# A spectral filter and a gated MLP in one kernel: the order of the first loads and the place of column 1's transposes

## The chip, the cores and the metric

The kernel runs on one core of a Trainium2 chip. The metric is device time in microseconds (us) of one execution; smaller is better. Each kernel is run several times and the median is given.

## The reference

What has to be computed, cut to its core (x is 2048 x 512 in bf16, w_gate and w_up are 512 x 1792, w_down 1792 x 512, w_r and w_i 2048 x 257):

```python
xn = _layernorm(x, axis=-1)
X = rfft2(xn); X = X * (w_r + 1j * w_i); a = irfft2(X)      # spectral branch
g = xn @ w_gate; u = xn @ w_up; b = (gelu_tanh(g) * u) @ w_down   # gated branch
return x + a + b
```

## The kernel before, in words

The 2048 rows are held as 16 "columns" of 128 rows: column c has the rows 16 p + c, p being the partition (`x_v`). For each column VectorE takes the statistics (`f_stats`, L337, `f_mean`, L340), the reciprocal root comes from ScalarE and VectorE for columns 0 and 1 and from GpSimd for the others, and the normalised xn goes to two places: transposed into `xnT` for the gated branch, and as it is into the spectral branch. Columns 0 to 3 are transposed on TensorE (`f_T`, L349) and copied from PSUM (`f_Tc`, L352); columns 4 to 15 are transposed by DMA (L450).

The gated branch is cut into units (`unit`). A unit has some columns and one to four blocks of 128 features: gate matmuls into `g_ps`, up matmuls into `u_ps`, a gelu on ScalarE (L498), a product on VectorE (L503) that writes `hT`. Each of the matmuls contracts 128 of the 512 inputs; e = 0..3 counts these. Units 0 and 1 are columns 0 and 1 with features 0 to 511, units 2 and 3 are columns 0 and 1 together with features 512 to 1023, then come columns 2 and 3, then all of columns 0 to 3 for the other features (`todo`). Unit 0 has its matmuls in halves over e, so that it can start on half of the weights (`mm_half`, L493); all other units are in `mm` (L485). Down products (`y_ps`, L815) make up the last third of the span. The spectral branch (`forward`, `group`, `inverse`: groups bp, dp, ep, gp, yp) is set between the units.

The order of the work on TensorE, VectorE, ScalarE, GpSimd and most of SyncE comes from a planner (`Plan.order`): each operation has an engine, an estimated length, what it depends on, a key (lower goes first when several could start), and in some cases an earliest time, `t_min`. The tables `LAND`, `WG_LAND` and `WU_LAND` give the planner such earliest times for the loads. Buffers are counted by names ("S", "G", "U" and so on: G and U have two PSUM buffers each, S has four). The planner only sets the order of instructions on each engine; on the chip they wait for each other by semaphores. The first loads and the filler matmuls are written out by hand in `opening`.

In `opening`, SyncE issues columns 0 and 1, four loads of the first up weights (features 0 to 511, one for each e), columns 2-3, the second gate and up weights (features 512 to 1023), columns 4-7, the third weights, columns 8-11, the table RF, columns 12-15, a small index table `idx_t` and constants. ScalarE issues the first gate weights in two halves. A DMA uses one of eight semaphores in turn, so the ninth load in order waits until the first has landed, the tenth until the second has, and so on. Column 0 goes through VectorE and TensorE (two transposes, filler matmuls L322, ScalarE's copies) to unit 0. Column 1 is made ready while unit 0 runs; its four transposes stand behind unit 0's up matmuls on TensorE, one VectorE copy takes all of them to `xnT`, and unit 1 comes next. ScalarE loads the gelu's table after the root of column 1. Of `first_two`, the statements for column 1's transposes:

```python
t = add("PE", 0.23, lambda: f_T(1, 0, NE), [o["xn1"]], key=-1998, lat=0.45, acq=("S",))
v("copyt", lambda: f_Tc(1, 0, NE), 0.5, ["t"])
xT_op[1] = o["copyt"]
return o["copyt"]
```

Of the kernel before, what the change touches and what calls it, by code (L numbers as in the profile page):

```python
# [21 lines left out]
NE = 4  # L22
# [179 lines left out]
def kernel(  # L202
# [50 lines left out]
    def load_x(c0, n, eng=nc.sync):  # L253
        eng.dma_start(out=x_t[:, c0:c0 + n, :], in_=x_v[:, c0:c0 + n, :])

    def load_w(a, b, eng=nc.sync):
        nc.sync.dma_start(out=Wg_sb[:, :, a:b], in_=wg_v[:, :, a:b])
        eng.dma_start(out=Wu_sb[:, :, a:b], in_=wu_v[:, :, a:b])
# [15 lines left out]
    def opening():  # L274
        nc.vector.memset(spin[:], 0.0)
        nc.vector.memset(eps_t[:], EPS)
        nc.vector.memset(minus_half[:], -0.5)
        U = nc.gpsimd
        U.memset(ident_t[:], 1.0)
        U.affine_select(out=ident_t[:], in_=ident_t[:], pattern=[[-1, P]], compare_op=ALU.is_equal, fill=0.0,  # L280
                        base=0, channel_multiplier=1)
        nc.scalar.activation(out=warm[:], in_=eps_t[:], func=AF.Sqrt, bias=eps_t[:], scale=1.0)
        load_x(0, 1)
        load_x(1, 1)
        load_w(Wg_sb, 0, 512, nc.scalar, e=slice(0, 2))
        load_w(Wg_sb, 0, 512, nc.scalar, e=slice(2, 4))
        for e in range(NE):
            load_w(Wu_sb, 0, 512, e=e)
        load_x(2, 2)
        load_w(Wg_sb, 512, 1024)  # L290
        load_w(Wu_sb, 512, 1024)
        load_x(4, 4)
        load_w(Wg_sb, 1024, DF)
        load_w(Wu_sb, 1024, DF)
        load_x(8, 4)
        nc.sync.dma_start(out=RF_t[:], in_=rf_d.rearrange("p (c k) -> p c k", c=NC))
        load_x(12, 4)
        nc.sync.dma_start(out=idx_t[:], in_=nc.inline_tensor(idx_np, name="spec_rows").ap())
        load_consts("F0", "L0")
        load_consts("I0", "M0")  # L300
        for T, w_in in ((TR, A_w_r), (TI, A_w_i)):
            rows = w_in.rearrange("(kb a h g) k -> h kb a (g k)", kb=NC, h=2, a=8)
            Tf = T.rearrange("p j k -> p (j k)")
            for h in range(2):
                nc.sync.dma_start(out=Tf[64 * h:64 * h + 64, W:8 * W], in_=rows[h, :, 0:4, W:8 * W])
        for k in range(37):
            nc.tensor.matmul(sp_ps[:, :P], lhsT=spin[:], rhs=spin[:], start=True, stop=True)  # L307

    LAND = {0: 2.9, 1: 4.5, 2: 7.2, 3: 7.2}
    LAND.update({c: 11.5 if c < 8 else 17.5 if c < 12 else 20.5 for c in range(4, NC)})  # L310
    WG_LAND = [5.0] * 4 + [8.6] * 4 + [13.2] * 6
    WU_LAND = [6.7] * 4 + [10.0] * 4 + [15.2] * 6
    RF_LAND = 19.0

    ident = ident_t[:]
# [35 lines left out]
    def f_Tc(c, e0, n, copy=V.tensor_copy):  # L351
        copy(out=xnT[0][:, e0:e0 + n, c, :], in_=tiles["T", c, e0][:])  # L352
# [14 lines left out]
        U.tensor_tensor(out=b, in0=mv[:, c0:c0 + n, 0], in1=rstd[:, c0:c0 + n], op=ALU.mult)  # L367
        U.tensor_scalar(out=b, in0=b, scalar1=-1.0, scalar2=None, op0=ALU.mult)  # L368

    xn_op, xT_op = {}, {}  # L370

    def first_two():
        o = {}

        def v(k, fn, occ, deps=(), lat=None, t_min=0.0):
            o[k] = add("DVE", occ, fn, [o[d] for d in deps], key=-2000 + len(o), lat=lat, t_min=t_min,
                       after=o.get("last"))
            o["last"] = o[k]

        def T(c, h):  # L380
            o["T", c, h] = add("PE", 0.12, lambda: f_T(c, 2 * h, 2), [o["xn", c, h]], key=-2000 + 2 * c + h,
                               lat=0.36, acq=("S",))

        def xn_(c, h):
            v(("xn", c, h), lambda: f_norm_v(c, 256 * h, 256), 0.27, [("recip", c)], lat=0.4)

        def stats(c):
            v(("stats", c), lambda: f_stats(c), 0.6, t_min=LAND[c], lat=0.7)

        def mean(c):  # L390
            v(("mean", c), lambda: f_mean(c), 0.17, [("stats", c)])
            o["root", c] = add("ACT", 0.31, lambda: A.activation(
                out=rstd[:, c:c + 1], in_=mv[:, c, 1:2], func=AF.Sqrt, bias=eps_t[:], scale=1.0),
                [o["mean", c]], key=-2000 + c)

        def recip(c):
            v(("recip", c), lambda: V.reciprocal(out=rstd[:, c:c + 1], in_=rstd[:, c:c + 1]), 0.15, [("root", c)])

        stats(0)
        mean(0)  # L400
        recip(0)
        xn_(0, 0)
        xn_(0, 1)
        stats(1)
        mean(1)
        T(0, 0)
        T(0, 1)
        add("PE", 0.33, spin_on, [o["T", 0, 1]], key=-1500, lat=0.33, after=o["T", 0, 1])
        table = add("ACT", 1.3, lambda: None, [o["root", 1]], key=-1500, lat=1.3)
        xT_op[0, 0], xT_op[0] = (  # L410
            add("ACT", 0.36, lambda h=h: f_Tc(0, 2 * h, 2, A.copy), [o["T", 0, h]], key=-1990 + h, lat=0.48,
                rel=("S",)) for h in range(2))
        recip(1)
        xn_op[0] = o["xn", 0, 1]
        v("xn1", lambda: f_norm_v(1, 0, D), 0.33, [("recip", 1)], lat=0.45)
        t = add("PE", 0.23, lambda: f_T(1, 0, NE), [o["xn1"]], key=-1998, lat=0.45, acq=("S",))
        o["t"] = t
        v("copyt", lambda: f_Tc(1, 0, NE), 0.5, ["t"])
        o["copyt"].rel = ("S",)
        xT_op[1] = o["copyt"]  # L420
        xn_op[1] = o["xn1"]
        return o["copyt"]

    ROOT = 1.1
    chain_end = first_two()
# [39 lines left out]
    def unit(k, c0, n, f0, m=1):  # L465
# [19 lines left out]
                    T_.matmul(b[name][:, f], lhsT=W_[:, e, (f0 + f) * P:(f0 + f + 1) * P], rhs=rhs[:, e, :],  # L485
                              start=(e == 0), stop=(e == NE - 1))

        def mm_half(s, name="g_ps", tag="G", W_=Wg_sb):
            if s == 0:
                b[name] = ps.tile([P, m, w], F32, name=name, tag=tag, bufs=2)  # L490
            for e in (2 * s, 2 * s + 1):
                for f in range(m):
                    T_.matmul(b[name][:, f], lhsT=W_[:, e, (f0 + f) * P:(f0 + f + 1) * P], rhs=rhs[:, e, :],  # L493
                              start=(e + f == 0), stop=(e == NE - 1), skip_group_check=True)
# [12 lines left out]
        def split(name, tag, W_, key, t, h):  # L507
# [3 lines left out]
                        lat=occ * h / m + 0.3, acq=() if f else (tag,), t_min=t[f0 + f + h - 1])  # L511
            return o

        if k == 0:
            g = add("PE", occ / 2, lambda: mm_half(0), [xT_op[0, 0]], key=1000, acq=("G",), t_min=WG_LAND[0])
            g = add("PE", occ / 2, lambda: mm_half(1), [xT_op[0], g], key=1000.1, lat=occ / 2 + 0.3)
            u = add("PE", occ / 2, lambda: mm_half(0, "u_ps", "U", Wu_sb), [g], key=1000.5, acq=("U",), t_min=6.2)
            u = add("PE", occ / 2, lambda: mm_half(1, "u_ps", "U", Wu_sb), [u], key=1000.6, lat=occ / 2 + 0.3,
                    t_min=WU_LAND[0])
        else:  # L520
            g = split("g_ps", "G", Wg_sb, 1000 + k, WG_LAND, m)
            u = split("u_ps", "U", Wu_sb, 1000.5 + k, WU_LAND, (2, m, 1)[k] if k < 3 else m)
        ge = add("ACT", {1: 0.28, 2: 0.36, 4: 0.5}[n * m], f_ge, [g], key=-1000 + k,
                 lat={1: 0.38, 2: 0.48, 4: 0.7}[n * m], acq=("ge",), rel=("G",))
        h = add("DVE", {1: 0.21, 2: 0.34, 4: 0.61}[n * m], f_h, [ge, u], key=-1000 + k, rel=("U", "ge"))
# [354 lines left out]
```

## Time and profile before

| What | us |
|---|---|
| Median of 6 runs | 178.9 (178.81 to 179.15) |
| The profiled execution, its own time | 178.81 |
| Its span in the profile | 177.1 |
| TensorE busy | 171.9 (97%) |
| VectorE busy | 115.6 (65%) |
| ScalarE busy | 96.4 (54%) |
| GpSimd busy | 17.1 (10%) |
| TensorE share of the chain that ended last | 95% |

The span goes from the first to the last instruction in the profile; the 1.7 us between it and the execution's time lie around it. The "chain" is the run of work that ended last, followed back from the last instruction to what released each step. A line of the chain has a start and a length in us, the engine, the tile written, the line of the kernel and how many instructions were merged. A line of the timeline has the same with shapes added, and in brackets how long the engine was idle before, and what ended the wait. SPq and ACTq are DMA issues on SyncE's and ScalarE's queues; "us to landing" of a DMA counts from the start of its issue to the moment at which a waiting engine can go on. TensorE ran at its full granted clock in the whole span by the page (clock tenths 9 throughout).

### The profile page before, as it was taken

What the parts mean: (1) busy time and instruction counts of PE and PEld (TensorE: products, weight loads), DVE (VectorE), ACT (ScalarE), POOL (GpSimd) and SP (SyncE); (2) the same over time, 40 slices, a digit from 0 to 9 for tenths busy, and PEclk for the clock granted to TensorE, in tenths of its full rate; (3) what the DMA queues carried; (4) which work ended last, traced back from release to release, by engine and by line L of the source; (5) the groups of instructions that cost most, each with busy time, mean ns of one, the idle gap of its engine ahead of it and who ended that gap; (6) DMA issues with size and microseconds to landing.
All of it is one profiled execution on the core that took longest, in us unless ns stands there. A gap on an engine that the chain in (4) does not pass through costs nothing.

```text
span 177.1 us, 3114 instructions
## 1 busy us (share of the span) xinstructions
PE 171.9 (97%) x1128; PEld 97.4 (55%) x1145; DVE 115.6 (65%) x253; ACT 96.4 (54%) x172; POOL 17.1 (10%) x38
## 2 busy tenths in 40 slices
PE   7999999999999999999999999999999999999993
PEld 7898845464545554555555444454445445444463
DVE  2588799988334599998799999543516325345333
ACT  4633389798745999799999955452112111211200
POOL 1020260406760000000000000000000000000000
PEclk9999999999999999999999999999999999999999
DMA  5999975543717802111201520200132221221212
GB/s 151 324 365 401 349 165 97 112 92 51 246 33 236 297 4 59 43 46 35 59 14 47 146 68 0 59 0 4 57 91 89 75 76 61 89 87 61 79 43 59
DMA packets 21359, 19.35 MB, mean 109 GB/s; under 512 B 8480, under 2 KB 20000, under 8 KB 21344
## 3 DMA queue, kind: packets, MB, share of 16 engines
q1 hardware_dynamic: 20384, 17.31, 33.3%
q0 software_dynamic: 416, 1.32, 2.6%
q10 hardware_dynamic: 544, 0.52, 1.1%
q8 instruction: 9, 0.15, 0.3%
q14 instruction: 6, 0.05, 0.1%
HBM read 13.38 MB, written 2.10 MB: 87 GB/s over the span
## 4 chain that ended last, share of the span: by engine, by line
PE 95%; DMA 1%; issue 1%; DVE 1%; SPq 0%
PE y_ps L815 27%; PE u_ps L485 27%; PE g_ps L485 25%; PE sp_ps L307 2%; PE yp L766 2%; PE bp L575 2%; PE dp L633 2%; PE y_ps L819 2%; PE gp L736 2%; PE ep L642 2%; DMA F<-F 1%; PE tp L349 1%; PE g_ps L493 1%; PE u_ps L493 1%; PE sp_ps L322 0%
## 5 line engine op out<-in xcount | busy, mean ns | idle before, releaser
L485 PE MATMUL u_ps<-xnT,Wu_sb 128*128 128x512 bf16 (+2 forms) x254 | 56.5, 349 | 0.3
L485 PE MATMUL g_ps<-xnT,Wg_sb 128*128 128x512 bf16 (+2 forms) x246 | 55.2, 348 | 0.8 <-DVE xnT L352 0.5
L815 PE MATMUL y_ps<-Wd_sb,hT 128*128 128x512 bf16 (+2 forms) x247 | 50.5, 355 | 0.2
L503 DVE TENSOR_TENSOR hT<-u_ps,ge 128x512 bf16<-128x512 f32 x56 | 38.5, 688 | 18.4 <-PE u_ps L485 14.1
L498 ACT ACTIVATE ge<-g_ps 128x512 bf16<-128x512 f32 x56 | 33.8, 604 | 22.0 <-PE g_ps L485 18.1
L815 PEld LDWEIGHTS <-hT 128*128 128x128 bf16 x252 | 23.2, 98 | 22.5
L485 PEld LDWEIGHTS <-Wu_sb 128*128 128x128 bf16 x256 | 24.0, 98 | 20.9
L485 PEld LDWEIGHTS <-Wg_sb 128*128 128x128 bf16 x256 | 23.8, 98 | 20.5 <-issue 0.6
L772 ACT CAST yf<-yp 128x512 bf16<-128x512 f32 x16 | 9.3, 586 | 40.5 <-PE yp L766 40.5
L822 DVE TENSOR_TENSOR y_sb<-y_ps,y_sb 128x512 bf16<-128x512 f32 (+2 forms) x18 | 11.1, 631 | 30.0 <-PE y_ps L819 30.0
L647 ACT CAST E<-ep 64x512 bf16<-64x512 f32 x32 | 18.5, 579 | 1.3 <-PE ep L642 0.8
L337 DVE BATCH_NORM_STATS2 stats<-x_t 128x6 f32<-128x512 bf16 x16 | 10.5, 678 | 3.0 <-DMA x_t<-in_A_x_dram 3.0
L447 ACT ACTIVATE xn<-x_t,nb,rstd 128x512 bf16<-128x512 bf16 x12 | 9.5, 814 | 2.1 <-POOL nb L368 2.1
L545 ACT CAST Gs<-gp 128x512 bf16<-128x512 f32 x16 | 9.0, 593 | 1.0 <-PE gp L736 0.9
L545 ACT CAST ds<-dp 128x512 bf16<-128x512 f32 x16 | 9.0, 598 | 0.6 <-PE dp L633 0.5
L545 ACT CAST Bs<-bp 128x512 bf16<-128x512 f32 x16 | 8.6, 608 | 0.5 <-PE bp L575 0.5
L778 DVE TENSOR_TENSOR lv<-yf 128x512 bf16<-128x512 bf16 x16 | 6.1, 421 | 1.5 <-ACT yf L772 0.6
L766 PEld LDWEIGHTS <-Gs 128*128 128x128 bf16 x64 | 4.8, 98 | 3.5
L785 DVE TENSOR_TENSOR yt<-lv 128x512 bf16<-128x512 bf16 x16 | 6.1, 422 | 0.3
L766 PE MATMUL yp<-CT,Gs 128*128 128x128 bf16 x64 | 6.0, 219 | 0.1
L819 PE MATMUL y_ps<-yt,RI_t 128*128 128x512 bf16 (+2 forms) x18 | 6.1, 355 | 0.0
L736 PEld LDWEIGHTS <-F 128*128 128x128 bf16 x64 | 4.5, 98 | 2.6
(67 smaller groups left out, 124.2 us busy)
## 6 DMA issues: line engine op xcount, KB each, us to landing
F<-F SPq DMA_DIRECT2D x32, 64.0 KB, 2.0
y_sb<-in_A_x_dram SPq DMA_DIRECT2D x16, 128.0 KB, 2.1
out_dram<-y_sb SPq DMA_DIRECT2D x15, 128.0 KB, 1.7
Wd_sb<-in_B_w_down_dram SPq DMA_DIRECT2D x1, 1792.0 KB, 7.9
x_t<-in_A_x_dram SPq DMA_DIRECT2D x3, 512.0 KB, 11.7
Wg_sb<-in_B_w_gate_dram SPq DMA_DIRECT2D x1, 768.0 KB, 9.0
Wu_sb<-in_B_w_up_dram SPq DMA_DIRECT2D x1, 768.0 KB, 10.5
Wg_sb<-in_B_w_gate_dram ACTq DMA_DIRECT2D x2, 256.0 KB, 3.8
```

The lines of the kernel that those rows point to most:

```text
L337: V.bn_stats(out=st[:], in_=x_t[:, c, :])
L447: xn_op[c] = add("ACT", 0.72, lambda c=c: A.activation(out=xn[:, c, :], in_=x_t[:, c, :], func=AF.Identity, bias=nb[:, c:c + 1], scale=rst ...
L485: T_.matmul(b[name][:, f], lhsT=W_[:, e, (f0 + f) * P:(f0 + f + 1) * P], rhs=rhs[:, e, :], start=(e == 0), stop=(e == NE - 1))
L498: A.activation(out=b["ge"][:], in_=b["g_ps"][:], func=AF.Gelu_apprx_tanh)
L503: V.tensor_tensor(out=hT_of(sb, f0, m, o, w), in0=b["u_ps"][:], in1=b["ge"][:], op=ALU.mult)
L545: A.copy(out=o, in_=i)
L647: A.copy(out=b["E"][64 * h:64 * h + 64, r], in_=b["ep", h][64 * r:64 * r + 64])
L766: T_.matmul(t[:, q], lhsT=late["G"][:, q, c0 + j], rhs=IQ[q], start=(q == 0), stop=(q == 3), skip_group_check=True)
L772: A.copy(out=b["yf"][:, j], in_=b[j][:])
L815: T_.matmul(b[o][:], lhsT=hT_of(sb, f, 1, cl * P, P)[:, 0], rhs=Wd_sb[:, f, o:o + w], start=(f == 0), stop=False)
L819: T_.matmul(b[o][:], lhsT=late["RI"][:, c, :], rhs=late["yt"][:, c, o:o + w], start=False, stop=True)
L822: V.tensor_tensor(out=b["y"][:, o:o + w], in0=b[o][:], in1=b["y"][:, o:o + w], op=ALU.add)
```

## The change

First, in `opening`: the first up weights go to ScalarE's queue, in two halves as the gate weights, and columns 2-3 behind them on that queue. SyncE issues columns 0 and 1, then `idx_t`, then the second gate weights. Ahead of that load GpSimd copies one element of column 0 to the first place that the load will write, so that the load waits for the copy, and the copy for column 0. Columns 8 to 15 come in four loads of two instead of two of four.

Second, in `first_two` and `unit`: column 1's transposes are in two pairs, and stand between the first and the second quarter of unit 0's up matmuls. VectorE copies the first pair, ScalarE the second pair, ahead of its table load. Unit 1's gate has halves over e too, so that its first half needs VectorE's copy only.

Third, the planner's landing estimates for columns 0 and 1 and for the up weights are other numbers.

```diff
--- before.py
+++ after.py
@@ -282,20 +282,22 @@
         nc.scalar.activation(out=warm[:], in_=eps_t[:], func=AF.Sqrt, bias=eps_t[:], scale=1.0)
         load_x(0, 1)
         load_x(1, 1)
-        load_w(Wg_sb, 0, 512, nc.scalar, e=slice(0, 2))
-        load_w(Wg_sb, 0, 512, nc.scalar, e=slice(2, 4))
-        for e in range(NE):
-            load_w(Wu_sb, 0, 512, e=e)
-        load_x(2, 2)
+        for T in (Wg_sb, Wu_sb):
+            for e in (0, 2):
+                load_w(T, 0, 512, nc.scalar, e=slice(e, e + 2))
+        load_x(2, 2, nc.scalar)
+        nc.sync.dma_start(out=idx_t[:], in_=nc.inline_tensor(idx_np, name="spec_rows").ap())
+        U.tensor_copy(out=Wg_sb[0:1, 0, 512:513], in_=x_t[0:1, 0, D - 1:D])
         load_w(Wg_sb, 512, 1024)
         load_w(Wu_sb, 512, 1024)
         load_x(4, 4)
         load_w(Wg_sb, 1024, DF)
         load_w(Wu_sb, 1024, DF)
-        load_x(8, 4)
+        load_x(8, 2)
+        load_x(10, 2)
         nc.sync.dma_start(out=RF_t[:], in_=rf_d.rearrange("p (c k) -> p c k", c=NC))
-        load_x(12, 4)
-        nc.sync.dma_start(out=idx_t[:], in_=nc.inline_tensor(idx_np, name="spec_rows").ap())
+        load_x(12, 2)
+        load_x(14, 2)
         load_consts("F0", "L0")
         load_consts("I0", "M0")
         for T, w_in in ((TR, A_w_r), (TI, A_w_i)):
@@ -306,10 +308,10 @@
         for k in range(37):
             nc.tensor.matmul(sp_ps[:, :P], lhsT=spin[:], rhs=spin[:], start=True, stop=True)
 
-    LAND = {0: 2.9, 1: 4.5, 2: 7.2, 3: 7.2}
+    LAND = {0: 2.65, 1: 4.6, 2: 7.2, 3: 7.2}
     LAND.update({c: 11.5 if c < 8 else 17.5 if c < 12 else 20.5 for c in range(4, NC)})
     WG_LAND = [5.0] * 4 + [8.6] * 4 + [13.2] * 6
-    WU_LAND = [6.7] * 4 + [10.0] * 4 + [15.2] * 6
+    WU_LAND = [6.4] * 4 + [10.2] * 4 + [15.2] * 6
     RF_LAND = 19.0
 
     ident = ident_t[:]
@@ -367,7 +369,7 @@
         U.tensor_tensor(out=b, in0=mv[:, c0:c0 + n, 0], in1=rstd[:, c0:c0 + n], op=ALU.mult)
         U.tensor_scalar(out=b, in0=b, scalar1=-1.0, scalar2=None, op0=ALU.mult)
 
-    xn_op, xT_op = {}, {}
+    xn_op, xT_op, between = {}, {}, {}
 
     def first_two():
         o = {}
@@ -413,13 +415,17 @@
         recip(1)
         xn_op[0] = o["xn", 0, 1]
         v("xn1", lambda: f_norm_v(1, 0, D), 0.33, [("recip", 1)], lat=0.45)
-        t = add("PE", 0.23, lambda: f_T(1, 0, NE), [o["xn1"]], key=-1998, lat=0.45, acq=("S",))
-        o["t"] = t
-        v("copyt", lambda: f_Tc(1, 0, NE), 0.5, ["t"])
-        o["copyt"].rel = ("S",)
-        xT_op[1] = o["copyt"]
+        o["t", 0] = add("PE", 0.12, lambda: f_T(1, 0, 2), [o["xn1"]], key=1000.54, lat=0.3, acq=("S",))
+        o["t", 1] = add("PE", 0.12, lambda: f_T(1, 2, 2), [o["xn1"]], key=1000.55, lat=0.3, acq=("S",),
+                        after=o["t", 0])
+        between.update(o)
+        v("copyt0", lambda: f_Tc(1, 0, 2), 0.25, [("t", 0)], lat=0.4)
+        o["copyt1"] = add("ACT", 0.4, lambda: f_Tc(1, 2, 2, A.copy), [o["t", 1], table], key=-1400)
+        o["copyt0"].rel = o["copyt1"].rel = ("S",)
+        xT_op[1, 0] = o["copyt0"]
+        xT_op[1] = o["copyt1"]
         xn_op[1] = o["xn1"]
-        return o["copyt"]
+        return o["copyt0"]
 
     ROOT = 1.1
     chain_end = first_two()
@@ -485,10 +491,10 @@
                     T_.matmul(b[name][:, f], lhsT=W_[:, e, (f0 + f) * P:(f0 + f + 1) * P], rhs=rhs[:, e, :],
                               start=(e == 0), stop=(e == NE - 1))
 
-        def mm_half(s, name="g_ps", tag="G", W_=Wg_sb):
-            if s == 0:
+        def mm_part(e0, e1, name="g_ps", tag="G", W_=Wg_sb):
+            if e0 == 0:
                 b[name] = ps.tile([P, m, w], F32, name=name, tag=tag, bufs=2)
-            for e in (2 * s, 2 * s + 1):
+            for e in range(e0, e1):
                 for f in range(m):
                     T_.matmul(b[name][:, f], lhsT=W_[:, e, (f0 + f) * P:(f0 + f + 1) * P], rhs=rhs[:, e, :],
                               start=(e + f == 0), stop=(e == NE - 1), skip_group_check=True)
@@ -511,15 +517,21 @@
                         lat=occ * h / m + 0.3, acq=() if f else (tag,), t_min=t[f0 + f + h - 1])
             return o
 
+        up = "u_ps", "U", Wu_sb
         if k == 0:
-            g = add("PE", occ / 2, lambda: mm_half(0), [xT_op[0, 0]], key=1000, acq=("G",), t_min=WG_LAND[0])
-            g = add("PE", occ / 2, lambda: mm_half(1), [xT_op[0], g], key=1000.1, lat=occ / 2 + 0.3)
-            u = add("PE", occ / 2, lambda: mm_half(0, "u_ps", "U", Wu_sb), [g], key=1000.5, acq=("U",), t_min=6.2)
-            u = add("PE", occ / 2, lambda: mm_half(1, "u_ps", "U", Wu_sb), [u], key=1000.6, lat=occ / 2 + 0.3,
-                    t_min=WU_LAND[0])
+            g = add("PE", occ / 2, lambda: mm_part(0, 2), [xT_op[0, 0]], key=1000, acq=("G",), t_min=WG_LAND[0])
+            g = add("PE", occ / 2, lambda: mm_part(2, NE), [xT_op[0], g], key=1000.1, lat=occ / 2 + 0.3)
+            u = add("PE", occ / 4, lambda: mm_part(0, 1, *up), [g], key=1000.5, acq=("U",))
+            between["t", 0].deps.append(u)
+            u = add("PE", occ / 4, lambda: mm_part(1, 2, *up), [u, between["t", 1]], key=1000.6)
+            u = add("PE", occ / 2, lambda: mm_part(2, NE, *up), [u], key=1000.7, lat=occ / 2 + 0.3, t_min=WU_LAND[0])
+        elif k == 1:
+            g = add("PE", occ / 2, lambda: mm_part(0, 2), [xT_op[1, 0]], key=1001, acq=("G",))
+            g = add("PE", occ / 2, lambda: mm_part(2, NE), [*src, g], key=1001.3, lat=occ / 2 + 0.3)
+            u = split(*up, 1001.5, WU_LAND, m)
         else:
             g = split("g_ps", "G", Wg_sb, 1000 + k, WG_LAND, m)
-            u = split("u_ps", "U", Wu_sb, 1000.5 + k, WU_LAND, (2, m, 1)[k] if k < 3 else m)
+            u = split("u_ps", "U", Wu_sb, 1000.5 + k, WU_LAND, 1 if k == 2 else m)
         ge = add("ACT", {1: 0.28, 2: 0.36, 4: 0.5}[n * m], f_ge, [g], key=-1000 + k,
                  lat={1: 0.38, 2: 0.48, 4: 0.7}[n * m], acq=("ge",), rel=("G",))
         h = add("DVE", {1: 0.21, 2: 0.34, 4: 0.61}[n * m], f_h, [ge, u], key=-1000 + k, rel=("U", "ge"))
```

## The prediction, made before the changed kernel ran

> **What bounds the kernel now.** First view: the page's busy shares and its chain. TensorE is busy 97% of the span and holds 95% of the chain that ended last, so time comes off only where TensorE waits. Second view: the chain from 5 us, which shows where that is.
>
> ```profile
> 5.60 0.64 PE sp_ps L322 x6
> 6.24 1.07 PE g_ps L493 x16
> 7.31 0.89 PE u_ps L493 x16
> 8.20 0.24 PE tp L349 x4
> 8.44 0.02 issue
> 8.46 0.44 DVE xnT L352
> 8.90 0.04 issue
> 8.94 1.05 PE g_ps L485 x16
> 10.00 0.89 PE u_ps L485 x16
> 10.89 0.87 PE g_ps L485 x8
> 11.76 0.87 PE u_ps L485 x8
> 12.64 0.45 PE tp L349 x8
> ```
>
> Columns: start, length, what. Between 8.44 and 8.94 TensorE has transposed column 1 and stands still until VectorE has copied it: 0.50 us. From 8.94 it never stops for more than 0.05 us until the tail. Ahead of 6.24 it runs filler matmuls (37, then 6), whose number is fixed, so an earlier column 0 gains nothing.
>
> Third view: SyncE's part of the timeline, with the times from issue to landing of the DMA list. Issue plus landing time gives when each load is usable.
>
> ```profile
> 3.60 0.43 SPq L266 DMA_DIRECT2D x_t<-in_A_x_dram  x1
> 4.74 0.39 SPq L270 DMA_DIRECT2D Wg_sb<-in_B_w_gate_dram  x1
> 5.93 0.38 SPq L270 DMA_DIRECT2D Wu_sb<-in_B_w_up_dram  x1
> ```
>
> ```profile
> Wg_sb<-in_B_w_gate_dram SPq DMA_DIRECT2D x1, 512.0 KB, 5.3
> Wu_sb<-in_B_w_up_dram SPq DMA_DIRECT2D x1, 512.0 KB, 5.6
> x_t<-in_A_x_dram SPq DMA_DIRECT2D x1, 256.0 KB, 4.5
> ```
>
> Columns 2-3 land at 3.60 + 4.5 = 8.1, the second gate weights at 4.74 + 5.3 = 10.04, the second up weights at 5.93 + 5.6 = 11.53. The chain needs the last two at 10.89 and 11.76: spare 0.85 and only 0.23 us. This is the number to keep: the stall hides a DMA that is nearly late too.
>
> Fourth view: VectorE and ScalarE in the same stretch.
>
> ```profile
> 8.81 1.28 DVE L337 BATCH_NORM_STATS2 stats<-x_t 128x6 f32<-128x512 bf16 x2
> 10.00 0.30 DVE L340 BATCH_NORM_AGGREGATE mv<-stats 128x2 f32<-128x6 f32 x2
> 10.22 1.48 DVE L503 TENSOR_TENSOR hT<-u_ps,ge 128x512 bf16<-128x512 f32 x2
> 11.61 0.73 DVE L343 TENSOR_SCALAR xn<-x_t,mv,rstd 128x512 bf16<-128x512 bf16 x2
> ```
>
> ```profile
> 6.28 1.28 ACT L498 ACT_TABLE_LOAD   x1
> 7.58 0.60 ACT L498 ACTIVATE ge<-g_ps 128x512 bf16<-128x512 f32 x1
> ```
>
> VectorE works without a gap from the statistics of columns 2-3 (8.81) to their normalised form (12.34); TensorE transposes them at 12.64 to 13.08, so that chain has about 0.2 us to spare: its last xn is ready 3.53 after the statistics start, then come a hand-over (0.06), four transposes (0.22) and their lag (0.3), so statistics that start at s let the transposes end at s + 4.1 at the earliest.
>
> **What the skill says.** "DMA: Bandwidth & Descriptors", section "Issuing engines are not separate DMA queues": loads issued from several engines run on the same 16 DMA engines; only issue time is saved. The trace agrees: the core's rate from 4 to 7 us is 338 to 384 GB/s, with both queues active at first and SyncE's alone later. Same page, "Queues, rings and completion order": each DMA engine takes the queues in turn, packet by packet. The packet records agree: from 3.5 to 5.0 us the SyncE queue moved 231 KB and the ScalarE queue 283, 45 to 55. So moving a load to the other queue doesn't give it more bandwidth, it decides with whom it shares. No other place of the skill is used.
>
> **The change part by part.**
>
> *Column 1 inside the first up unit.* The same 4 transposes now follow 4 of the 16 up matmuls: 7.31 + 4 x 0.056 = 7.53, so they end at 7.77. xn of column 1 is ready at 6.91, 0.6 before. The copy is in two halves: VectorE's (the 512-wide one took 0.42, a half on ScalarE 0.33; I take 0.3) from 7.79 to 8.1, ScalarE's from 7.8 to 8.13. Meanwhile TensorE has 12 up matmuls left: 7.77 + 0.67 = 8.44. Gate of unit 1 starts there and not at 8.94: **-0.50 us**, hidden by those 0.67 us. If Wu e=2..3 is late the cover stretches with the stall.
>
> *ScalarE's copy ahead of the table load.* The load moves from 6.28 to 8.13-9.41; the first gelu ends at 10.02 and not at 8.18. Behind it wait the second gelu (10.6), the first product on VectorE (10.05, was 10.22, so no later) and the PSUM slot of unit 2's gate, wanted at 10.89 - 0.50 = 10.39: 0.3 spare. Cost 0; if the copy were 0.4 later, it would show on TensorE.
>
> *Two up weights, then columns 2-3 on ScalarE's queue.* Three more issues of about 0.48 after 2.03 end at 3.46; the next ScalarE work is at 3.92. Cost 0. They are issued at 2.0, 2.5, 3.0 instead of 1.71 to 3.60, behind the same bytes. Wu e=2..3 is wanted at 8.0 (landed 6.9 before).
>
> *idx_t first.* SyncE has it as third load: 1.5 KB in 128 rows. Its packets took 9 ns each, so 128/16 x 9 = 0.07 us of each DMA engine at least; at most as long as preparing 128 rows of any load: the first packet of column 1 came 0.92 us after that of the 256-row Wg load issued before it, hence 0.46 for 128 (estimate). All later loads move by 0.07 to 0.46.
>
> *The hold.* The GpSimd copy of one element: the same shape at L597 took 0.70 us. It waits for column 0 (2.97), so SyncE's gate load goes out at about 3.8, instead of 4.74; behind it on SyncE are all later loads, each of them before held by an older load's semaphore anyway. Queued on GpSimd behind it is the root of columns 2-3 (10.39), long after. The earlier issue can close the dip at 7 to 8 us (239 GB/s against about 370): up to 0.33 us earlier for what follows. But it can also share with Wu and columns 2-3: see the second rival.
>
> *x in pairs (8-15), key changes in the planner.* These columns are wanted from 13.7 on by VectorE and at 33 by TensorE: 0. On TensorE the order of some units with bp, dp, ep groups changes further on (the compiled order of both kernels shows it); every group stays between units of 0.87 us, and no stall over 0.05 shows there now: -0.1 to +0.5, taken as 0.
>
> **Sum.** Unit 2's up starts at the later of 11.76 - 0.50 = 11.26 and the landing of the second up weights, 11.53 shifted by -0.26 (dip closed, cheap idx) to +0.46. I take +0.05, as both effects are of like size: 11.58. The stall goes, and 0.32 of it comes back as a wait for Wu. Gain 11.76 - 11.58 = 0.18. The chain of columns 2-3 allows it: landing at 8.1 to 8.5, transposes end at 12.6 at best; TensorE's own end 12.90. TensorE is full after that, so the 0.18 lasts. The profiled execution took 178.81, span 177.1 plus 1.7 outside, unchanged: 178.63. The median of the runs is 178.90, 0.09 above: **178.7** (178.72).
>
> **Rivals.** *Full gain*: the dip closes and idx costs little; Wu lands at 11.27, 0.49 to 0.50 come off: 178.4. For: GpSimd frees SyncE 0.9 us earlier. Against: the DMA engines are already over 90% busy in all but that one microsecond.
>
> *Columns 2-3 come late (slower)*: with the gate load on SyncE's queue from about 3.8 + 1.05 = 4.9 (column 0: issue 0.80, first packet 1.84), ScalarE's queue gets 55% of 366 KB/us = 201. Up to 4.9, 552 of its 1,280 KB are through; the rest needs 3.6 us: 8.5, plus 0.5 to 0.75 from last data to usable: 9.0 to 9.3. Then the transposes end at 9.25 + 4.1 = 13.35 instead of 13.08: +0.27, with Wu e=2..3 about 7.9, just in time: 179.2, up to 179.5. It decides from a landing of 9.0. For: the 45 to 55 sharing. Against: column 1, issued at 1.22, moved nothing until 3.24, while a ScalarE load issued before it did: loads seem to be prepared in order of issue, and then the gate load stays behind columns 2-3.
>
> *The new order further on* exposes a wait at a group (ScalarE is over 95% busy from 80 to 100 us): +0.5, 179.4.
>
> **Numbers.** Forecast 46%, full gain 19%, columns 2-3 late 25%, later order 10%. A measurement tells about 0.2% (0.36 us) from no change: faster is below 178.54, slower above 179.26. Faster: 0.14 x 46 + 0.9 x 19 = 24%. Slower: 0.03 x 46 + 0.6 x 25 + 0.9 x 10 = 25%, and 3 more for the unpriced waits: 28%. Same: 48%. The range takes the full gain less a little (178.35) to the late columns with +0.45 (179.35).
>
> **What would show it.** Right: gate of unit 1 at about 8.44 with no wait for xnT; a gap of 0.2 to 0.4 before unit 2's up, ended by the Wu DMA; statistics of column 2 by 8.5. Wrong: gap before Wu e=2..3 (7.99), statistics waiting for the x DMA past 9.0, or a gate of unit 2 waiting for gelu; gaps on TensorE past 20 us.

## The result and the profile after

| | before | after |
|---|---|---|
| Median, us | 179.12 (178.60 to 180.02, 69 executions) | 179.67 (178.91 to 180.72, 32) |
| Ratio, 95% interval | 1 | 1.003 (1.002 to 1.0039) |
| The profiled execution, us | 178.81 | 179.51 |
| Its span, us | 177.1 | 177.5 |
| Execution less span, mean of all executions, us | 1.70 | 1.95 |

The changed kernel is slower by 0.54 us (0.003 x 179.12), where 0.18 less was forecast. The last row says that 0.25 of it lies outside the span; the other 0.29 is inside. The two profiled executions differ by more, 0.4 in the span: that of the kernel before is a quick one, 0.31 below its median. Inside, the chain of the changed kernel, followed back from 14 us:

```profile
4.86 7.13 DMA Wu_sb<-in_B_w_up_dram
11.99 0.05 issue
12.04 1.05 PE u_ps L491 x8
13.08 0.45 PE tp L351 x8
```

Before, this stretch was TensorE all the way but for the copy of `xnT`. Now one load, the second up weights, fills it from its issue at 4.86 to 11.99. The chain has the up matmuls of unit 2 at 12.04 where they stood at 11.76, and 1.05 long where they were 0.87. That is two ways of counting: behind another group the chain counts a group only from the end of the one ahead, which it overlaps; after a wait it counts all of it. TensorE's timeline, which counts every group from its own start, has the group 1.04 and 1.05 long, from 11.60 before and from 12.04 after:

```profile
11.60 1.04 PE L485 MATMUL u_ps<-xnT,Wu_sb 128*128 128x256 bf16 x8
```

So the group is late by 0.44, and the transposes of columns 2-3 end at 13.53 and not at 13.08. From the start of this group to TensorE's last matmul it is 162.5 us in both kernels, and in all runs below but e7, e10 and e11: what is lost ahead of this start is the loss. The timeline of the changed kernel has the waits in brackets:

```profile
8.07 0.62 PE L499 MATMUL u_ps<-xnT,Wu_sb 128*128 128x128 bf16 x8 [0.33 <-DMA Wu_sb<-in_B_w_up_dram]
8.52 1.06 PE L499 MATMUL g_ps<-xnT,Wg_sb 128*128 128x128 bf16 x16
10.60 1.03 PE L491 MATMUL g_ps<-xnT,Wg_sb 128*128 128x256 bf16 x8
12.04 1.05 PE L491 MATMUL u_ps<-xnT,Wu_sb 128*128 128x256 bf16 x8 [0.40 <-DMA Wu_sb<-in_B_w_up_dram]
```

The wait for `xnT` is gone, as meant. In its place are two waits for DMAs, one for the second half of the first up weights and one for the second up weights. A third gap, 0.13 us ahead of unit 2's gate at 10.60, has no releaser in the profile; the second gate weights land just before it. SyncE's timeline and the list of DMAs (last column: us from issue to landing) give the landings:

```profile
3.43 0.40 SPq L270 DMA_DIRECT2D Wg_sb<-in_B_w_gate_dram  x1
4.86 0.38 SPq L270 DMA_DIRECT2D Wu_sb<-in_B_w_up_dram  x1
```

```profile
Wg_sb<-in_B_w_gate_dram SPq DMA_DIRECT2D x1, 512.0 KB, 7.1
Wu_sb<-in_B_w_up_dram SPq DMA_DIRECT2D x1, 512.0 KB, 7.1
...
x_t<-in_A_x_dram ACTq DMA_DIRECT2D x1, 256.0 KB, 6.1
```

The second weights are issued 1.3 and 1.1 us earlier than before and land 0.5 and 0.4 later: 3.43 + 7.1 = 10.53 and 4.86 + 7.1 = 11.96. (The chain, which is exact, has 11.99 for the last; the list rounds to 0.1.) Columns 2-3 (issued at 3.10) land at 9.20, 1.1 later. The windows of both kernels show it in sums (first columns: window, its length, TensorE busy; last: DMA share, GB/s), first before, then after:

```profile
4.50:6.50 2.00, 2.00 (x22) 2.00 (x20) 1.50 (x6) 1.05 (x4) 0.00 (x0) 1.00 1.10 385
6.20:13.10 6.90, 6.38 (x95) 6.05 (x93) 4.67 (x12) 3.34 (x6) 0.97 (x2) 1.00 1.00 333
13.10:20.00 6.90, 6.90 (x65) 6.19 (x64) 5.27 (x13) 2.77 (x5) 0.00 (x0) 1.00 1.05 398
```

```profile
4.50:6.50 2.00, 2.00 (x28) 1.64 (x26) 1.57 (x6) 0.92 (x3) 0.00 (x0) 1.00 1.08 322
6.20:13.10 6.90, 6.04 (x86) 5.19 (x84) 4.29 (x11) 3.55 (x6) 0.97 (x2) 1.00 1.04 363
13.10:20.00 6.90, 6.90 (x69) 6.22 (x67) 5.64 (x14) 2.70 (x5) 0.00 (x0) 1.00 1.05 384
```

TensorE's idle time between 6.2 and 13.1 us goes from 0.52 to 0.86, which is the three gaps (0.33, 0.13, 0.40). The DMA rate is lower in the first window and higher in the second, and from 13.1 us TensorE is busy throughout in both kernels.

### The profile page after: what moved, and what is told of

The parts are those of the page before. It is cut to its first block, busy times and chain, and to the rows that moved or that the text cites. A ratio compares the mean times of both kernels' runs of the same rounds, so it can differ in the third digit from the quotient of the medians.

```text
span 177.5 us, 3118 instructions
## 1 busy us (share of the span) xinstructions
PE 171.9 (97%) x1127; PEld 96.7 (54%) x1145; DVE 115.7 (65%) x253; ACT 96.9 (55%) x173; POOL 17.4 (10%) x39
## 4 chain that ended last, share of the span: by engine, by line
PE 91%; DMA 6%; issue 1%; SPq 0%; DVE 0%
PE y_ps L827 27%; PE u_ps L491 26%; PE g_ps L491 26%; DMA Wu_sb<-in_B_w_up_dram 4%; PE gp L748 2%; PE yp L778 2%; DMA x_t<-in_A_x_dram 2%; PE bp L587 2%; PE dp L645 2%; PE y_ps L831 2%; PE ep L654 2%; PE tp L351 0%; SPq L266 0%; DVE y_sb L834 0%
## 5 line engine op out<-in xcount | busy, mean ns | idle before, releaser
L491 PE MATMUL u_ps<-xnT,Wu_sb 128*128 128x512 bf16 (+2 forms) x248 | 55.6, 348 | 0.8 <-DMA Wu_sb<-in_B_w_up_dram 0.4
L491 PE MATMUL g_ps<-xnT,Wg_sb 128*128 128x512 bf16 (+1 forms) x236 | 55.0, 357 | 0.3
L491 PEld LDWEIGHTS <-Wg_sb 128*128 128x128 bf16 x240 | 23.0, 98 | 20.8 <-issue 0.3
L569 DVE TENSOR_TENSOR A<-xn 128x1024 bf16<-128x1024 bf16 x8 | 5.2, 676 | 1.0 <-ACT xn L453 1.0
```

## The experiments

Each run changes the kernel before or after in one part. A ratio is to the kernel before, run beside it on the same chip. "Outside" is the execution less its span. "End" is the time from VectorE's last product (`y_sb`) to the last instruction of the profiled execution. "Rest" is the ratio's difference in us less what these two differ from 1.70 and 2.45: an estimate of what happens in the work itself. A ratio is known to 0.2 to 0.5 us either way, so small entries mean little. Issue and landing times are those of one profiled execution each, to 0.05 us, and it can lie far from the median (e10: 182.20 against 180.33; e9: 179.28 against 179.95).

| Kernel | Ratio (95%) | Outside, us | End, us | Rest, us | Second gate, up issued | Columns 2-3 land | Second up lands |
|---|---|---|---|---|---|---|---|
| before | 1 | 1.70 | 2.45 | 0 | 4.74, 5.93 | 8.10 | 11.53 |
| after | 1.003 (1.002 to 1.0039) | 1.95 | 2.45 | +0.29 | 3.43, 4.86 | 9.20 | 11.96 |
| e1 | 0.9985 (0.9975 to 0.9996) | 1.70 | 2.45 | -0.27 | 5.03, 6.18 | 7.90 | 11.78 |
| e2 | 1.0023 (1.0011 to 1.0035) | 1.96 | 2.45 | +0.15 | 3.87, 4.66 | 8.41 | 11.66 |
| e4 | 1.0023 (1.0003 to 1.0043) | 1.96 | 2.45 | +0.15 | 3.26, 3.69 | 10.31 | 12.69 |
| e6 | 1.0032 (1.0019 to 1.0045) | 1.71 | 2.57 | +0.44 | 3.20, 3.70 | 8.99 | 12.00 |
| e9 | 1.0045 (1.0034 to 1.0056) | 1.72 | 2.57 | +0.67 | 3.20, 3.68 | 8.79 | 11.88 |
| e7 | 1.0055 (1.0036 to 1.0074) | 2.12 | 2.57 | +0.44 | 5.52, 7.05 | 8.09 | 12.45 |
| e11 | 1.0001 (0.9984 to 1.0019) | 1.71 | 2.45 | 0 | 4.94, 6.31 | 8.00 | 11.51 |
| e17 | 0.9993 (0.9969 to 1.0017) | 1.70 | 2.45 | -0.13 | 5.09, 6.93 | 8.28 | 12.03 |
| e13 | 0.998 (0.9965 to 0.9994) | 1.71 | 2.52 | -0.44 | 4.08, 5.15 | 8.40 | 11.25 |
| e16 | 1.0009 (0.9992 to 1.0026) | 1.70 | 2.57 | +0.04 | 3.63, 4.11 | 9.03 | 12.01 |
| e14 | 0.9957 (0.994 to 0.9973) | 1.71 | 2.52 | -0.85 | 4.08, 5.27 | 8.10 | 11.17 |
| e10 | 1.0071 (1.0048 to 1.0094) | 1.71 | 2.57 | +1.14 | first of each 4.64, 7.30 | 7.90 | 12.88 |
| e12 | 1.003 (1.0016 to 1.0044) | 1.97 | 2.89 | -0.17 | 4.86, 5.73 | 8.12 | 12.03 |
| e3 | 1.0073 (1.0046 to 1.01) | 1.96 | 2.87 | +0.63 | 5.84, 6.28 | 7.95 | 12.08 |
| e15 | 1.003 (1.0016 to 1.0044) | 1.96 | 2.89 | -0.16 | 5.43, 6.61 | 8.19 | 12.71 |
| e18 | 1.0005 (0.999 to 1.0021) | 1.98 | 2.89 | -0.63 | 5.98, 6.43 | 8.36 | 11.83 |
| e19 | 1.0003 (0.9992 to 1.0014) | 1.74 | 2.89 | -0.43 | 4.01, 5.32 | 8.07 | 11.02 |
| e20 | 0.9993 (0.9974 to 1.0012) | 1.74 | 2.89 | -0.61 | 4.15, 5.35 | 7.90 | 11.35 |

The end goes with the number of DMAs. SyncE ends the kernel by waiting for the eight semaphores one after the other, in a fixed order. The timelines of the waits show that the one for the last store ends 1.5 to 1.6 us after the last product in every run, and that each wait that still stands behind it takes another 0.06. With 104 DMAs in the rotation, as before and after, the last store has the eighth semaphore (End 2.45; the profiles have 2.44 to 2.46); with 103 the seventh (2.52), with 102 or 110 the sixth (2.57), with 105 the first (2.89), with 106 the second (2.87). Here the last product and SyncE's last ten waits (when the first of them is over, and when the last), before and in e12, which has one DMA more than the changed kernel:

```profile
174.35 0.29 DVE y_sb L822
L875 SPq EVENT_SEMAPHORE  x10: 17/28/28, 175.1 to 177.0; - x10
```

```profile
174.80 0.29 DVE y_sb L836
L889 SPq EVENT_SEMAPHORE  x10: 17/28/28, 176.6 to 177.9; - x10
```

In the code below, `...` and angle brackets stand for what is left out.

### Computing or loads

e1 is the changed kernel with `opening` and the landing estimates of before; e2 the reverse; e4 is the changed kernel with the index load at its old place:

```diff
 e4
-        nc.sync.dma_start(out=idx_t[:], ...)
         U.tensor_copy(out=Wg_sb[0:1, 0, 512:513], in_=x_t[0:1, 0, D - 1:D])
...
         load_x(14, 2)
+        nc.sync.dma_start(out=idx_t[:], ...)
```

> The compute half of the change alone: column 1's transposes inside the first up unit, the two half copies and unit 1's gate in halves; loads and landing estimates as before. Theory (the new load order lost the time): the 0.50 us stall for xnT goes, the second up weights still land at about 11.5, and TensorE waits for them some 0.2 to 0.3 us at unit 2's up: 0.15 to 0.3 us faster than before. Rival (the moved transposes, the later table load or the new order further on cost the time themselves): equal to before or up to 0.5 us slower.

> The load half of the change alone (all first weights and columns 2-3 on ScalarE's queue, idx first, the hold, x in pairs, landing estimates of after), computation as before. Theory (loads): second up weights usable at about 12.0 as in the changed kernel, first up weights' second half at about 8.0; unit 2's up starts at about 12.0 instead of 11.76, so 0.2 to 0.4 us slower than before, no better than the changed kernel by over 0.2. Rival (compute half): equal to before within 0.1 us, as the 0.5 us stall for xnT covers late loads.

> The changed kernel with the load of idx_t back behind x (12-15). Theory that idx takes the loads' time (its 128 rows are prepared ahead of the up weights): first up weights' second half, columns 2-3 and second weights all usable 0.2 to 0.45 us earlier, TensorE's two waits for Wu shrink by as much: 0.2 to 0.4 us faster than the changed kernel. Rival (the shape of the up loads, or one queue working alone, sets the lower rate from 4.5 to 7 us): landings move by less than 0.1, time within 0.1 us of the changed kernel.

The computing is a gain of 0.27 us, the loads are a loss of 0.41 us alone, 0.26 of it outside the span. They do not add to 0.54: under the new computing the loads cost 0.54 + 0.27 = 0.81, of which 0.25 lies outside the span. The reading for this is that the new computing wants the second up weights half a microsecond earlier. In the profiled executions of all twelve kernels that have it and load these weights at once, unit 2's up starts 0.04 to 0.05 us after they land. Taking the index load from the front is no cure (1.0023), but e4 does not clear it either: the second up load then goes out 1.2 us earlier still, at 3.69.

### One edit of the loads that gives the whole loss

```diff
 e6 (to before) and e9 (to e1)
-        for e in range(NE):
-            load_w(Wu_sb, 0, 512, e=e)
+        for e in (0, 2):
+            load_w(Wu_sb, 0, 512, e=slice(e, e + 2))
```

> The kernel before with one edit: the first up weights in two loads of two e each instead of four of one, still on SyncE. Theory that the shape sets the lower rate (about 150 KB per half us for two e at once against 186 for one): what follows lands 0.2 to 0.5 us later, the rate from 5 to 7 us falls to about 150 KB per half us, and the kernel is 0.1 to 0.4 us slower through unit 2's up. Rival (the queue, or idx): landings and time as before within 0.1 us; with two issues fewer the second weights are issued earlier, which could even give 0.1 back.

> The change's computing with the loads of before, but for the first up weights in two loads on SyncE. Theory (that one edit of the loads is the whole loss, and it adds to the gain of the computing part): -0.27 us from the computing and +0.57 us from the two loads, +0.30 us, ratio 1.0017 (about 179.6 us), the same as the change as a whole. Rival (the queue, columns 2-3 on ScalarE or the hold carry the loss in the change as a whole, and the computing part hides the two loads): ratio below 1.000, near the 0.9985 of the computing alone.

With everything on its old queue, the first up weights in two loads cost 0.57 us, and 0.81 + 0.27 = 1.08 under the new computing: more than expected. Of each, 0.12 is the end. SyncE's timeline of e6, and its chain:

```profile
3.20 0.46 SPq L270 DMA_DIRECT2D Wg_sb<-in_B_w_gate_dram  x1
3.70 0.51 SPq L270 DMA_DIRECT2D Wu_sb<-in_B_w_up_dram  x1
```

```profile
3.70 8.30 DMA Wu_sb<-in_B_w_up_dram
12.00 0.05 issue
12.05 1.05 PE u_ps L485 x8
```

Two loads fewer ahead free two places in the rotation of eight semaphores: the second up weights are issued 2.2 us earlier and land half a microsecond later, as in the changed kernel. So either the cut into two or the early issue does the harm.

```diff
 e7 (to e6)
+        U.tensor_copy(out=Wg_sb[0:1, 0, 512:513], in_=x_t[0:1, 1, D - 1:D])
+        U.tensor_copy(out=Wu_sb[0:1, 0, 512:513], in_=Wu_sb[0:1, 0, 0:1])
         load_w(Wg_sb, 512, 1024)
 e11 (to e6) and e17 (to e9)
         for e in (0, 2):
             load_w(Wu_sb, 0, 512, e=slice(e, e + 2))
+            nc.sync.dma_start(out=<128 x 3 of pad_t>, in_=<1.5 KB>)
```

> The kernel before with the first up weights in two loads of two e, and two GpSimd copies that hold the second gate load until column 1 has landed (about 4.7 us) and the second up load until up slices e=0..1 have landed (about 6.5 us). Pacing theory (two loads fewer let the second weights be issued about 1.5 us earlier, so that fast DMA engines run ahead while the slowest lags): the second up weights land near 11.5 us again and the ratio to before is 1.000, at most 1.001 (about 179.3 us). Shape theory (two loads of 256 KB are themselves slower to complete than four of 128 KB): first up e=2..3 usable after 7.3 us, second up weights near 12.0 us, ratio 1.002 to 1.003 (about 179.7 us).

> The kernel before with the first up weights in two loads of two e, each followed by a load of 1.5 KB into a tile of its own, so that the number of loads ahead, the places in the rotation of eight semaphores and the times of issue stay those of before (columns 2-3 at about 3.6 us, second gate load at 4.7, second up load at 5.9). Pacing theory (what harms is that the second weights are issued some 2 us earlier when two loads are missing ahead of them): columns 2-3 land near 8.1 us and the second up weights near 11.5, ratio to before 1.000 to 1.001 (179.0 to 179.2 us). Shape theory (a load of 256 KB completes later than two of 128 KB, whenever the rest is issued): ratio 1.002 to 1.004, second up weights near 12.0.

> The change's computing, and the loads of before with the first up weights in two loads on SyncE, each followed by a load of 1.5 KB. Against the changed kernel with one tiny load it differs in the queue that the first up weights and columns 2-3 are issued on, at nearly the same times of issue of the second weights (4.9 and 6.3 us). Theory that ScalarE's queue makes no difference and the cut in two does the harm: ratio 1.002 to 1.004. Rival, on SyncE the cut in two is harmless if the second weights are issued at these times, and what is left of the loss is that of ScalarE's queue: ratio 0.998 to 1.000.

e7 missed: its holds let the loads out at 5.52 and 7.05, later than before, and the transfers fell to 213 to 305 GB/s from 8.5 to 11.5 us. It tells that late is bad too. e11 and e17 put the times right: the loss is gone, 1.0001 against 1.0032 and 0.9993 against 1.0045, with the cut left in two. So on SyncE's queue the early issue does it and not the cut. All loads behind are issued earlier too, columns 4-7 at 4.95 in e6 where it was 6.35, and no run parts these from the second weights. (e17's interval reaches to 1.0017; its profiled execution has the second up weights out at 6.93.) The medians show this, e11's profiled execution does not: at 179.62 it is slower than that of e6 (179.37), though unit 2's up starts at 11.67 without a wait. Columns 8-11 landed at 20.25 in it, VectorE stood still for 1.99 us ahead of their statistics, and TensorE waited 0.59 for a product at 21.61. Late loads can cost there too.

```diff
 e13 (to before) and e14 (to e1)
-        load_w(Wg_sb, 0, 512, nc.scalar, e=slice(0, 2))
-        load_w(Wg_sb, 0, 512, nc.scalar, e=slice(2, 4))
+        load_w(Wg_sb, 0, 512, nc.scalar)
 e16 (to e13)
-        for e in range(NE):
+        for e in (0, 1, slice(2, 4)):
             load_w(Wu_sb, 0, 512, e=e)
```

> The kernel before with the first gate weights in one load of 512 KB in place of two, the first up weights still in four: one load fewer ahead, so that the second gate load is issued at about 3.6 us and the second up load at about 4.9, as in the changed kernel. The first gate weights should be there by 5.9 us, before their first use at 6.0, so that the merging itself costs under 0.1 us. Pacing theory: columns 2-3 land near 8.9 us, second up weights near 12.0, ratio 1.002 to 1.003 (about 179.5 us). Shape theory: columns 2-3 near 8.1, second up weights near 11.5, ratio 1.000 to 1.001.

> The kernel before with the first gate weights in one load and the first up weights in three (one e, one e, two e): two loads fewer ahead than before, so that the second gate load is issued at about 3.6 us and the second up load at about 4.1, 0.5 to 1.0 us earlier than with one load fewer. Theory that issuing the second weights this early is what harms: columns 2-3 land near 8.9 us, second up weights near 11.9, ratio 1.002 to 1.003. Rival, only the cut of the first weights matters, and two loads in place of one pair of 128 KB costs little: columns 2-3 near 8.4, second up weights near 11.3, ratio 0.998 to 0.9995.

> The change's computing with the loads of before, but for the first gate weights in one load of 512 KB. If the gain of the computing (0.27 us, measured alone) and that of one load fewer ahead (0.36 us, measured alone: second up weights at 11.25 us in place of 11.53) add up: 178.5 us, ratio 0.9965. If both remove the same thing (the wait of typical executions for the second up weights): ratio 0.998, as either alone.

One load fewer (0.7 to 0.8 us earlier) is not a loss but a gain of 0.36 us, against both theories of that run; one more (another 0.5 and 1.0) gives it back, at 1.0009. There is a best time, then: second up weights issued at 5.1 to 5.4 us landed at 11.0 to 11.4 in four kernels; issued before 4.9, at 11.7 to 12.7 in six; after 5.7, at 11.5 to 12.9. (The four all have the first gate weights in one load; with two, no kernel issued at these times. One load is not enough: e15, e16 and e18 have it too and land at 11.8 to 12.7.) e14 beats both kernels: a median of 178.60 us against 179.14, its two gains adding up. Its chain has no DMA in it from 5 us on, though unit 2's up, at 11.19, still starts just as its weights land (11.17):

```profile
8.43 0.89 PE g_ps L496 x16
9.32 0.89 PE u_ps L488 x16
10.22 0.95 PE g_ps L488 x8
11.16 0.03 issue
11.19 1.05 PE u_ps L488 x8
```

e10 tried finer cuts of the second weights under the new computing:

```diff
 e10 (to e1)
-        load_w(Wg_sb, 512, 1024)
-        load_w(Wu_sb, 512, 1024)
+        for T in (Wg_sb, Wu_sb):
+            for e in range(NE):
+                load_w(T, 512, 1024, e=e)
```

> The change's computing with the loads of before, and the second gate and up weights each in four loads of one e (128 KB) in place of one of 512 KB. If many small paced loads keep the 16 DMA engines level: second up weights complete at 11.5 us or before in place of 11.8, columns 4-7 later by about 1 us but not before they are needed, ratio 0.997 to 0.998 (about 178.8 us). Rival (the bytes ahead set the landing, not the cut): ratio 0.9985 as with the computing alone. If columns 4-7 come too late for their statistics: over 1.000.

None of its three cases: slower by 1.27 us. Each of the eight loads waits in the rotation for an older one, they go out between 4.64 and 9.15 us, and the engines run dry (115 GB/s from 11.5 to 12.0). The profiled execution is an outlier: TensorE's granted clock was 0.75 in it from 13.1 to 20 us.

### Back to the changed kernel

```diff
 e12 (to after)
         nc.sync.dma_start(out=idx_t[:], ...)
+        nc.sync.dma_start(out=pad_t[:], in_=<1.5 KB>)
 e3 (to after)
-        for T in (Wg_sb, Wu_sb):
-            for e in (0, 2):
-                load_w(T, 0, 512, nc.scalar, e=slice(e, e + 2))
+        for e in (0, 2):
+            load_w(Wg_sb, 0, 512, nc.scalar, e=slice(e, e + 2))
+        for e in range(NE):
+            load_w(Wu_sb, 0, 512, nc.scalar, e=e)
 e15 (to e3)
-        for e in (0, 2):
-            load_w(Wg_sb, 0, 512, nc.scalar, e=slice(e, e + 2))
+        load_w(Wg_sb, 0, 512, nc.scalar)
 e18 (to e15): the index load at its old place, and
-        U.tensor_copy(out=Wg_sb[0:1, 0, 512:513], in_=x_t[0:1, 0, D - 1:D])
+        U.tensor_copy(out=Wg_sb[0:1, 0, 512:513], in_=x_t[0:1, 1, D - 1:D])
 e19 (to e18)
-        U.tensor_copy(out=Wg_sb[0:1, 0, 512:513], in_=x_t[0:1, 1, D - 1:D])
+        for k in range(4):
+            U.tensor_copy(out=Wg_sb[0:1, 0, 512:513], in_=x_t[0:1, 0, D - 1 - k:D - k])
 e20 (to e19): first up weights and columns 2-3 on SyncE
```

> The changed kernel with one more load of 1.5 KB after that of the indices on SyncE, which takes a place in the rotation: the second gate load then waits for column 1 (about 4.8 us in place of 3.4), the second up load goes out at about 5.7 in place of 4.9. Pacing theory: columns 2-3 land near 8.3 us in place of 9.2, second up weights near 11.6 in place of 12.0, ratio to before about 0.999 to 1.000 (the computing part's gain comes through). Shape theory, or ScalarE's queue being the cause: ratio stays 1.002 to 1.004.

> The changed kernel with the first up weights in four loads of one e on ScalarE's queue and without the GpSimd write; all else as changed. With four loads there are eight loads before columns 2-3, so that each later load waits for an early one's semaphore. Theory (the two loads in place of four are the loss): second up weights usable near 11.6 us, ratio 0.9985 to 0.9995 (about 179.1 us). Rival (ScalarE's queue, or columns 2-3 on it, is the loss): second up weights near 12.0 us, ratio 1.002 to 1.003.

> The changed kernel with the first gate weights in one load and the first up weights in four, all still on ScalarE's queue ahead of columns 2-3; the indices and the GpSimd write as changed. Theory that the way the early loads are cut (and with it, when the second weights are issued) is the whole loss: second up weights near 11.5 us, ratio 0.997 to 0.999. Rival, ScalarE's queue with all first weights and columns 2-3 in it is a loss of its own: second up weights near 12.0, ratio 1.002 to 1.004, as with the change itself.

> The changed kernel with the first gate weights in one load and the first up weights in four, all on ScalarE's queue with columns 2-3; the load of the indices back at its old place, so that it takes no place in the rotation and its landing at 5.7 to 6.6 us no longer releases the second up load; the GpSimd write waits for column 1, so that the second gate load goes out at about 5.0 us and the second up load at about 5.5. Theory that the times of issue and the cut are all: second up weights near 11.4 us, ratio 0.996 to 0.999. Rival, ScalarE's queue ahead of columns 2-3 costs 0.4 us or more by itself: second up weights near 12 us, ratio 1.002 to 1.004.

> The changed kernel with the first gate weights in one load, the first up weights in four, all on ScalarE's queue with columns 2-3, the load of the indices at its old place, and four GpSimd copies in a row after column 0 has landed, so that the second gate load goes out at about 4.1 us and the second up load at about 5.2, when column 1 has landed: the times of issue of the fastest kernel so far (ratio 0.9957), from which it then differs in the queue of the up weights and of columns 2-3. Theory that the times of issue are all: second up weights near 11.2 to 11.5 us, ratio 0.9955 to 0.9985. Rival, ScalarE's queue costs by itself: second up weights at 11.8 us or later, ratio 1.000 to 1.003.

> The run before (all first weights in the good cut and columns 2-3 on ScalarE, four GpSimd copies, 178.7 us in its profiled execution but a ratio of 1.0003 over its executions) with one edit: the first up weights and columns 2-3 issued on SyncE. All else, the semaphores of the second weights and the order of the computing included, is the same. Theory that ScalarE's queue costs by itself in the typical execution: ratio 0.9955 to 0.998. Rival, the GpSimd copies, the tail of the x loads in twos or the chip were the difference from the fastest kernel: ratio 0.999 to 1.001, as on ScalarE.

The text on e3 is wrong in one point: it kept the GpSimd write. e3 is worse, because with nine loads ahead columns 2-3 wait for a semaphore on ScalarE until 4.85, and ScalarE's root of column 0 behind them: unit 0's gate starts at 6.90, where it started at 5.92.

By the ratios, neither the later issue alone (e12) nor the other cut alone (e15) mends the changed kernel: 1.003 as before. But both have 105 DMAs and pay 0.44 us at the end. The rest is -0.17 in e12 and -0.16 in e15, where it is +0.29 in the changed kernel and -0.27 with the computing alone. So the later issue alone takes back about 0.46 of the 0.56 us that the loads cost in the work: an estimate, good to 0.3 either way by the two intervals. By this estimate the pacing theory of e12 holds in the work, and the total hides it. No trace shows it: e12's profiled execution, 180.01 where the median is 179.57, has the landing at 12.03 as the changed kernel has. In that of e15 (180.70, median 179.66) the chain goes through the index load, which takes a place in the rotation: it landed at 6.60, 4.89 us after its issue, and let the second up load out only at 6.61.

With that place free, the hold on column 1 and the other cut (e18), 0.45 us come back (1.0005 against 1.003). e18, e19 and e20 have 105 DMAs too; their rest is -0.63, -0.43 and -0.61, and what keeps the ratios near 1 is the end, in e18 the time outside as well. e20 changes the queue alone: 1.0003 and 0.9993, intervals overlapping. ScalarE's queue is no cause that these runs can see. This agrees with what the Trainium skill says in "DMA: Bandwidth & Descriptors", section "Issuing engines are not separate DMA queues". Both stay above e14, with second weights issued within 0.1 us of its times. For e20 that is 0.0036 or 0.64 us: 0.37 is the end, 0.03 the time outside, and 0.24 is left, which the intervals do not tell from none. It may lie in the four copies, the pairs of x loads, the landing estimates or the chip. e19's profiled execution was the fastest of its 14, so its 11.02 is not typical.

## Why the prediction was wrong, point by point

- *Column 1 inside the first up unit*: right. VectorE's copy took 0.29 (0.3 taken), ScalarE's 0.37 (0.33), no wait is left, and e1 measures a gain of 0.27. The 0.50 is even too small, as a gate without a wait also takes 0.89 in the chain and not 1.05: in e14 unit 1's gate ends at 9.32, where it ended at 10.00.
- *ScalarE's copy ahead of the table load, issues on ScalarE*: right, cost 0. *idx_t first*: not measured by itself, as e4 also moves the issue times.
- *The hold*: the copy took 0.18, not 0.70, so that the load went out at 3.43, not 3.8. In the sum the earlier issue stands as a gain (-0.26); only a rival has it as a harm. The dip did close, from 250 GB/s to 307 between 6.5 and 8 us, but another opened (385 to 322 between 4.5 and 6.5), and what had to come first came later.
- *Sum, the landing of the second up weights* is the step that failed: 11.53 shifted by -0.26 to +0.46, taken +0.05, "as both effects are of like size". It was +0.43, and the first effect gave nothing. Start of unit 2's up: 12.04 instead of 11.58; the half of the first up weights added a wait of 0.33 at 8.07. The step priced bytes and preparation, but not the time of issue. That it was a matter of issue is shown on SyncE's queue (e6 against e11, e9 against e17); in the changed kernel e12 gives it 0.46 of the loads' 0.56 us (0.29 + 0.27), by estimate. How the cut and the index load's place share what is left is not settled.
- *"Gain 11.76 - 11.58"* failed beside it: it sets a start after a wait against the end of the group ahead. By the timeline the group started at 11.60 before, and with a landing at 11.58 it would have started at 11.62 or 11.63. So the forecast of 0.18 was none by its own landing. The base was off too: 178.90 was the median of 6 executions, 179.12 is that of 69.
- *"span 177.1 plus 1.7 outside, unchanged"* failed too: 1.95, 0.25 us of the loss. It goes with the GpSimd write: the seven kernels with one copy have 1.95 to 1.98, the ten without have 1.70 to 1.72, and e7, which adds nothing but two copies to e6, has 2.12 where e6 has 1.71. The changed kernel without the write was not run.
- *Rival, columns 2-3 late*: landing 9.0 to 9.3 forecast, 9.20 measured, with the sharing at another time, so the agreement is part luck. By the packet records the gate load, issued at 3.43, moved nothing until 6.2, 2.8 us later, where 4.9 was priced. From 4.5 to 6.2 ScalarE's queue was alone, with 535 KB. Then they did share: up to 8.75 SyncE's queue moved 424 KB and ScalarE's its last 367. Nor was it the columns that bound: their transposes stood behind the late up matmuls.
- *Rival, new order further on*: no. From the start of unit 2's up to the last matmul TensorE takes 162.5 us in both.

What the early issue does inside the DMA engines is seen in part only. When columns 2-3 landed, the two queues had moved 274 KB beyond the 1,536 KB up to their end in the kernel before, but 566 in the changed one, 534 in e6, 404 in e9, 462 in e16 and 922 in e4. e13 and e14, the fastest, have 394 and 332, so the count goes with the time of issue but does not by itself tell harm. In part the data was slower: at 8.0 us the changed kernel had moved 1,693 KB, the kernel before 1,779; by 11 us they were level. For the most part it was other data: from 7.75 to 8.75 us the last 30 KB of columns 2-3 trickled in, while SyncE's queue moved 296 KB. Read as DMA engines out of step, some were far into the second weights while another still had a part of columns 2-3. The Trainium skill says in "DMA: Bandwidth & Descriptors", section "Why a DMA increments its semaphore by 16 and not by 1", that the engines of a DMA finish independently and are counted, so that a load is as late as its last engine; these bytes agree. Why one falls behind is open: the records do not name the DMA engines.

## What to carry to other kernels

Cutting or joining early loads also moves every later load in the rotation of semaphores: read the times of issue of the loads behind, and try one load more and one fewer. The number of loads also sets how many waits stand behind the last store, here up to 0.44 us: take that out before a small difference is put down to the early loads. Issue early enough that the engines do not run dry, and not so early that urgent data is overtaken; here the best place was some 6 us ahead of the landing. When a stall is removed that hid a nearly late DMA, the landing becomes the bound, and the sum should take it from the late end of its range.

## What the runs showed that was not expected

- A 1.5 KB load issued third took 4.0 to 4.9 us to land (after, e15), about as long as the 256 KB loads around it. A place in the rotation behind such a load is a long wait.
- The time outside the span differs by 0.13 us at most between a kernel's executions and its mean, and goes with the number of GpSimd copies added, but not in proportion: 1.70 for none, 1.96 for one, 2.12 for two (e7), 1.74 for four (e19, e20). From e18 to e19 only the copies are edited, and 0.24 us go. What it is, the profile does not show.
